# Attention's products by heads in column groups, an output stage with tokens on the rows, and other prices in the planner

## The chip, the cores and the metric

The kernel runs on one core of a Trainium2 chip. That core has TensorE (PE, matrix products into PSUM banks), VectorE (DVE), ScalarE (ACT), GpSimd (POOL) and the queue that issues DMA (SP). The metric is the device time of one execution in microseconds, the median of several runs; lower is better.

## The reference

Three stages follow each other: attention with 8 heads over 4 sequences of 512 local and 32 global tokens, a feed-forward layer, and a layer of 8 experts that all tokens pass through, weighted by a balanced gate.

```
s_g = scale * q_g @ k_all.T                    # global tokens see all
s_l = [scale * q_l @ k_g.T, where(|i-j| <= 32, scale * q_l @ k_l.T, -1e9)]
x = concat(softmax(s_g) @ v_all, softmax(s_l) @ v_all)      # 2176 tokens x 512
x = maximum(x @ w_in, 0) ** 2 @ w_out                       # 512 -> 2048 -> 512, float64 weights
P = exp(x @ w_gate - max); 8 times: rows / sum, columns / sum, * N / E
out = sum over e of P[:, e] * (maximum(x @ w1[e], 0) @ w2[e])   # 8 experts, 512 -> 1024 -> 512
```

## The kernel before

The 2176 tokens are 17 tiles of 128, in three blocks of 5, 6 and 6 tiles. Layer 0 is the feed-forward layer in 4 units of 512 hidden features, layer 1 the experts in 16 units (two an expert). A block passes through all units of a layer, then the next block does: 20 units for block 0, 40 for blocks 1 and 2.

Each product of float32 matrices is made of three products of float32r parts (a rounded part and the rest, `split_terms`). A unit has two halves. The hidden half makes hidden features from tokens by a scheme of seven products in place of eight on 2x2 blocks (Strassen-Winograd): `H(i, q)`, 14 groups of six products, 384 columns wide in blocks 1 and 2, 320 in block 0. The groups with bank a0 or a1 add up in one bank, and each is copied away (by ACT to `snaps`, or by DVE) before the next is added. `done` makes the hidden values. The output half differs:

- Block 0, `plain_unit`: it takes all eight blocks, works out the forms of the weights itself (`own_w1`, `own_w2`, on DVE, POOL and ACT) and stores them in HBM for the other blocks. In layer 1 the hidden values are the weights of the array, so a row of the result is a token, and DVE multiplies it by the token's probability while it adds it to `acc`.
- Blocks 1 and 2, `later_unit`: it loads the stored forms, makes forms of the hidden values (`form`, `combine`; s1 and s2 on DVE, s3 and s4 on POOL) and runs seven products by `O(name)`, each as two groups of six products of 384 columns, with tokens along the columns (turned). DVE adds each into `acc`. In layer 1 the hidden values are multiplied by the probabilities in `done`, since a column can't be scaled by a number per row; `turn_prob` turns the probabilities, writes them to HBM, and one DMA an expert spreads them over the rows (tile `tw1`). `send` turns each output tile back on PE at the end of a block.

Attention goes over 16 pairs of heads. `local` does two query tiles of a pair: scores with 64 rows a head, on the two halves of the array's rows, softmax on DVE, ACT and POOL, transposes, and the product with the values, in which one product of 256 columns makes both heads by each head's values and a half of the result is not used. `glob` does the global tokens of two pairs. `convert` turns the float64 words of `w_in` and `w_out` into float32 by integer operations on ACT, DVE and POOL and is run beside attention.

The order of all this is not written by hand. A `Recorder` takes every call with its operands, `cost` gives it a duration, and `plan` lists the operations by critical path on a model of the engines; what is emitted is each engine's list in that order. All instructions are therefore recorded with the recorder's line (L79, L84 in the changed kernel), and tiles name them: `a`, `b`, `d`, `y` are PSUM banks, `xf` and `c` the forms of tokens and of hidden weights, `xh` and `zs` hidden values (probabilities in attention), `wide` and `snaps` results on the way, `w`, `r`, `tw` output weights, `acc` the tokens.

## Time and profile before

| | |
|---|---|
| median of 3 runs (lowest, highest) | 2043.98 us (2042.07, 2045.91) |
| profiled execution, its span | 2047.04 us, 2045.3 us |
| PE busy | 1945.5 us, 95% of the span, 11008 products |
| weight loads (PEld) busy | 1828.0 us, 89% |
| DVE busy | 1722.7 us, 84%, 3171 instructions |
| ACT busy | 1003.2 us, 49% |
| POOL busy | 820.7 us, 40% |
| mean granted TensorE clock | 0.984 |

Busy PE time is modelled, and products overlap: the distance between starts, or a count in a stretch, says more than the duration of one. Durations of DVE and ACT instructions overlap by a little too. A product of float32 (in attention and the gate) leaves two records, one of float32r leaves one.

### The profile page before, as it was taken

How to read it: one execution, taken by the hardware profiler on the slowest of the kernel's cores; microseconds unless marked ns; L12 is line 12 of the kernel's file. 1: busy time of each engine (PE TensorE's matmuls, PEld its weight loads, DVE VectorE, ACT ScalarE, POOL GpSimd, SP SyncE). 2: the span in 40 equal slices, each digit the busy share in tenths (PEclk: the TensorE clock that was granted, in tenths of full speed). 3: DMA queues.
4: the chain of work that ended last, by engine and by line, in shares of the span. 5: the costliest groups of instructions: out<-in, count | busy, mean ns of one | idle time of the engine just before them, and what ended most of it. 6: DMA issues, size and time to landing. Idle time of an engine off the chain costs nothing.

```text
span 2045.3 us, 32874 instructions
## 1 busy us (share of the span) xinstructions
PE 1945.5 (95%) x11008; PEld 1828.0 (89%) x11008; DVE 1722.7 (84%) x3171; ACT 1003.2 (49%) x2319; POOL 820.7 (40%) x843
## 2 busy tenths in 40 slices
PE   7899999999988999999999999999999999999998
PEld 5677889999986888888889999999999999999998
DVE  4788998676798878888878899889899889989987
ACT  5788755676564444554445333333334433433432
POOL 4466653333352545455434233323323323333331
PEclk8999999999989999999999999999999999999999
DMA  8877789666635888788898777777676767677763
GB/s 194 225 200 202 237 272 326 223 219 227 226 127 192 275 296 281 266 275 273 299 308 273 238 233 235 245 228 234 232 234 222 250 233 253 217 244 234 234 225 103
DMA packets 335930, 486.21 MB, mean 238 GB/s; under 512 B 91400, under 2 KB 252168, under 8 KB 335760
## 3 DMA queue, kind: packets, MB, share of 16 engines
q1 hardware_dynamic: 335760, 484.10, 72.8%
q8 instruction: 87, 1.43, 0.3%
q14 instruction: 83, 0.68, 0.1%
HBM read 351.03 MB, written 128.24 MB: 234 GB/s over the span
## 4 chain that ended last, share of the span: by engine, by line
PE 55%; DVE 27%; DMA 5%; issue 4%; ACT 2%; POOL 1%; SPq 0%; DVEq 0%; ACTq 0%; POOLq 0%
PE y L79 26%; PE a L79 14%; PE d L79 10%; DVE wide L79 10%; DVE xh L79 8%; PE b L79 5%; DMA r<-in_moe_w_dram 2%; DVE xf L79 2%; DVE zs L79 2%; DVE r L79 2%; DVE acc L79 1%; DVE c L79 1%; ACT xh L79 1%; DMA w2forms<-xf 1%; DVE ss L79 1%
## 5 line engine op out<-in xcount | busy, mean ns | idle before, releaser
L79 PE MATMUL a<-xf,c 128*128 128x384 f32 (+1 forms) x2880 | 549.4, 333 | 35.9 <-DVE zs L79 20.6
L79 PEld LDWEIGHTS a<-xf,c 128*128 128x128 f32 x2880 | 486.5, 191 | 55.8 <-DVE zs L79 25.3
L79 ACT CAST xh<-wide 128x384 fp32r<-128x384 f32 x480 | 239.1, 514 | 348.2 <-DVE wide L79 278.0
L79 POOL TENSOR_TENSOR c<-r,c 128x256 fp32r<-128x256 f32 (+1 forms) x160 | 185.9, 1166 | 550.5 <-ACT c L79 512.4
L79 POOL TENSOR_TENSOR wide<-wide 128x384 f32<-128x384 f32 (+1 forms) x192 | 248.2, 1298 | 286.3 <-DVE xh L79 72.0
L79 DVE TENSOR_TENSOR xh<-wide,xh 128x384 fp32r<-128x384 f32 x480 | 325.8, 700 | 34.5 <-ACT xh L79 34.5
L79 PE MATMUL d<-xf,c 128*128 128x384 f32 (+1 forms) x1440 | 277.6, 329 | 0.3 <-DMA c<-w1forms 0.2
L79 DVE TENSOR_TENSOR acc<-y,acc 128x384 f32<-128x384 f32 (+2 forms) x401 | 214.4, 548 | 41.2 <-PE y L79 40.4
L79 PEld LDWEIGHTS d<-xf,c 128*128 128x128 f32 x1440 | 244.1, 189 | 1.1 <-DVE wide L79 0.5
L79 PE MATMUL y<-w,xh 128*128 128x512 f32 x960 | 222.7, 392 | 1.0 <-DVE acc L79 1.0
L79 PE MATMUL y<-xh,w 128*128 128x384 f32 (+1 forms) x1104 | 206.6, 331 | 13.1 <-DVE xh L79 10.1
L79 PEld LDWEIGHTS y<-w,xh 128*128 128x128 f32 x960 | 180.4, 189 | 38.4 <-DVE acc L79 1.4
L79 ACT CAST c<-r 128x512 fp32r<-128x512 f32 (+1 forms) x240 | 121.0, 512 | 175.7 <-PE b L79 151.0
L79 PEld LDWEIGHTS y<-xh,w 128*128 128x128 f32 x1104 | 182.3, 189 | 25.4 <-DVE xh L79 22.3
L79 DVE SCALAR_TENSOR_TENSOR wide<-wide,tw 128x384 f32<-128x384 f32 x192 | 182.2, 951 | 4.3
L79 PE MATMUL b<-xf,c 128*128 128x384 f32 (+1 forms) x720 | 139.2, 328 | 0.8 <-DVE wide L79 0.8
L79 PE MATMUL y<-xh,r 128*128 128x384 f32 x720 | 139.5, 335 | 0.0
L79 ACT COPY snaps<-a 128x384 f32<-128x384 f32 (+1 forms) x240 | 109.9, 458 | 49.5 <-PE a L79 42.8
L79 POOL TENSOR_TENSOR w<-r,w 128x512 fp32r<-128x512 f32 x40 | 54.5, 1364 | 197.5 <-ACT w L79 129.7
L79 PEld LDWEIGHTS y<-xh,r 128*128 128x128 f32 x720 | 126.1, 188 | 0.0
L79 PEld LDWEIGHTS b<-xf,c 128*128 128x128 f32 x720 | 121.5, 188 | 1.2 <-DVE wide L79 1.2
L79 ACT CAST w<-r 128x512 fp32r<-128x512 f32 x80 | 47.9, 621 | 146.0 <-PE y L79 123.2
(154 smaller groups left out, 3220.7 us busy)
## 6 DMA issues: line engine op xcount, KB each, us to landing
c<-w1forms SPq DMA_DIRECT2D x160, 512.0 KB, 4.4
w<-w2forms SPq DMA_DIRECT2D x160, 512.0 KB, 4.3
r<-in_moe_w_dram SPq DMA_DIRECT2D x128, 512.0 KB, 4.8
w1forms<-c SPq DMA_DIRECT2D x80, 512.0 KB, 5.3
w2forms<-xf SPq DMA_DIRECT2D x160, 256.0 KB, 4.2
r<-w2forms SPq DMA_DIRECT2D x80, 512.0 KB, 4.3
w2forms<-w SPq DMA_DIRECT2D x240, 128.0 KB, 4.1
tw<-w2forms SPq DMA_DIRECT2D x40, 512.0 KB, 4.4
```

The costliest lines, as they stand in the source:

```text
L79: getattr(getattr(self.nc, eng), name)(*args, **kwargs)
```

## The change

Five things change.

1. In attention the product with the values makes each head by itself: `local` runs pairs of products of 128 columns, one with its result on PSUM rows 0 to 63 and one on 64 to 127; `glob` does the same by pairs of heads in the scores and by four heads in the product with the values. The result is then one block, and one eviction on DVE moves it, where an eviction by ACT and one by DVE moved the halves.
2. The output half of `later_unit` in layer 1 has tokens on the rows, as block 0 has: `O_tokens` with products of 256 columns. DVE multiplies by the probability at the eviction. `turn_prob`, its DMAs and the transposes of `send` go, and ACT alone makes the hidden values.
3. s3 and s4 of `later_unit` are on DVE, in both layers.
4. One cast of `convert` goes from ACT to POOL (32 times).
5. The planner: `cost` says of each operation whether it uses the port that DVE and POOL share, and `listed` lengthens two that overlap; durations of DVE, ACT and POOL count 1.05 times, a DMA lands 4 us later, grouped products side by side count a half or a quarter, and there are four rounds for three.

```diff
+        for op in self.ops:
+            if op.eng == "sync":
+                op.lat += LATER
+            elif op.eng in ("vector", "scalar", "gpsimd"):
+                op.dur *= SLOWER
+        order, _, _ = plan(self.ops)
...
+        op.dur = dur * {"heads": 0.5, "scores": 0.5, "heads4": 0.25}.get(tag, 1.0) + (0.25 if tag else 0.0)
...
+        if not psum and name in ("tensor_scalar", "tensor_copy", "memset"):
+            return 0.15 + 0.00053 * n, 0.09, 0, True
+        d = 0.149 + 0.00105 * n
+        if name == "scalar_tensor_tensor" and psum and n == 512:
+            d += 0.06
+        return d, 0.09, 0, kinds.count("SB") > 1
     if name in ("tensor_scalar", "memset", "tensor_copy", "affine_select"):
-        return 0.33 + 0.00056 * n, 0.09, 0
-    return 0.25 + 0.0023 * n, 0.09, 0
+        return 0.33 + 0.00053 * n, 0.09, 0, True
+    return 0.19 + 0.00215 * n, 0.09, 0, True
...
+SLOWER, LATER = 1.05, 4.0
...
+def slowed(dur, beside, eng):
+    if beside <= 0:
+        return dur
+    rate = 0.64 if eng == "vector" else 0.78
+    return dur / rate if dur <= beside * rate else dur + beside * (1 - rate)
...
+        if nodes[i][3]:
+            d = slowed(d, held["gpsimd" if e == "vector" else "vector"] - t, e)
+            held[e] = t + d
...
-        act.activation(out=up, in_=lower, func=AF.Copy, scale=2.0**-29)
+        pool.tensor_scalar(out=up, in0=lower, scalar1=2.0**-29, scalar2=0.0, op0=mul, op1=add)
...
+            pv = pv_bank()[:, 0 : 2 * P].rearrange("p (t n) -> p t n", t=2)
+            with nc.group("heads"):
                 for t in range(2):
                     qt = 2 * qp + t
                     for y, (a, c) in enumerate(((va[:, qt], ta[:, t]), (vb[:, qt], tb[0:96, t]))):
...
-                        pe.matmul(pv[:, t].rearrange("p j q -> p (j q)"), lhsT=a, rhs=c, start=(y == 0), stop=(y == 1))
-            c0 = b * SL + qp * 2 * P
-            for j, r in enumerate(halves):
-                eng = (act, dve)[j]
-                if block_of(c0 // P) == block_of(c0 // P + 1):
-                    blk = block_of(c0 // P)
-                    o = c0 - TBS[blk][0] * P
-                    dst = turned_block(blk)[r, p, o : o + 2 * P].rearrange("p (t q) -> p t q", t=2)
-                    move(eng, dst, pv[r, :, j, :])
-                else:
-                    for t in range(2):
-                        token_out(p, r, c0 + t * P, P, pv[r, t, j, :], eng)
+                        for j, r in enumerate(halves):
+                            pe.matmul(pv[r, t], lhsT=a[:, r], rhs=c[:, j], start=(y == 0), stop=(y == 1))
...
+            token_out(p, b * SL + qp * 2 * P, 2 * P, pv.rearrange("p t n -> p (t n)"), dve)
...
+            with nc.group("heads"):
+                for i in range(2):
+                    kt, o = KT[(n - 1 + i) % 3], slice(i * 2 * SG, (i + 1) * 2 * SG)
+                    w = bd[:, i].rearrange("p j s -> p (j s)")
+                    pe.matmul(sa[o], lhsT=w, rhs=kt[:, 0, 0 : P + SG], start=True, stop=True)
...
+            with nc.group("heads4"):
                 for y, (a, m) in enumerate(terms):
-                    pe.matmul(pv.rearrange("p h d -> p (h d)"), lhsT=a, rhs=m, start=(y == 0), stop=(y == len(terms) - 1))
+                    for h in range(4):
+                        i, j = divmod(h, 2)
+                        o = slice(h * SG, (h + 1) * SG)
+                        pe.matmul(pv[o], lhsT=a[:, o], rhs=m[:, i, halves[j]], start=(y == 0), stop=(y == len(terms) - 1))
...
-        pbc = TW[1].get(F32)[:, 0 : 2 * n]
-        if layer and u % UE == 0:
-            k = (tb - 1) * 2 * n
-            sp.dma_start(out=pbc, in_=turned_prob[e : e + 1, k : k + 2 * n].partition_broadcast(P))
...
+            act.activation(out=dst, in_=src, func=AF.Relu)
             if layer == 0:
-                act.activation(out=dst, in_=src, func=AF.Relu)
                 act.activation(out=dst, in_=dst, func=AF.Square)
-            else:
-                dve.scalar_tensor_tensor(
-                    out=dst, in0=src, scalar=0.0, in1=pbc[:, half * n : (half + 1) * n], op0=ALU.max, op1=mul
-                )
...
+            if layer:
+                return O_tokens(name, fm, wf)
...
+        def O_tokens(name, fm, wf):
+            for t in range(nj // 2):
+                z, w = bank[f"y{t}"], bank[("b", "d0", "d1")[t]]
+                ps = {"T1": w[:, HALF:DM], "B22": w[:, HALF:DM], "B21": w[:, 0:HALF]}.get(fm, z[:, 0:HALF])
+                with nc.group():
+                    k = 0
+                    for q in range(2):
+                        for lhs, rhs in split_terms(
+                            *(hidden_form(name, x, q)[:, t * P : (t + 1) * P] for x in range(2)), *(wf[:, x, q] for x in range(2))
+                        ):
+                            pe.matmul(ps, lhsT=lhs, rhs=rhs, start=(fm in ("B11", "T1") and k == 0), stop=(k == 5), skip_group_check=True)
+                            k += 1
+                if fm == "B21":
+                    continue
+                i, c, src = {
+                    "B11": (0, 0, ps), "T1": (1, 1, ps), "T2": (0, 1, ps), "T3": (1, 1, ps), "B22": (0, None, w), "T4": (1, 0, ps),
+                }[fm]
+                j = j0 + i * (nj // 2) + t
+                dst, pr = acc_t[:, j] if c is None else acc_t[:, j, c * HALF : (c + 1) * HALF], prob[:, j, e : e + 1]
+                if u == 0 and fm in ("B11", "T1", "T2", "T4"):
+                    dve.tensor_scalar(out=dst, in0=src, scalar1=pr, scalar2=None, op0=mul)
+                else:
+                    dve.scalar_tensor_tensor(out=dst, in0=src, scalar=pr, in1=dst, op0=mul, op1=add)
+                if u == NU[1] - 1 and fm in ("B22", "T4"):
+                    send(j)
...
-        s3 = lambda: combine("A11", "A21", sub, pool)
-        s4 = lambda: combine("A12", "A22", sub, pool)
+        s3 = lambda: combine("A11", "A21", sub, dve)
+        s4 = lambda: combine("A12", "A22", sub, dve)
...
+    def send(j):
+        if j * P < GL:
+            b, r = divmod(j * P, SL)
+            sp.dma_start(out=out[b * S + SG + r : b * S + SG + r + P], in_=acc_t[:, j])
+        else:
+            for b in range(B):
+                sp.dma_start(out=out[b * S : b * S + SG], in_=acc_t[b * SG : (b + 1) * SG, j])
...
-    def turn_prob():
-        for k in range(0, rest, 4):
-            nt = min(4, rest - k)
-            ps = y_bank()[0:E, 0 : nt * P]
-            with nc.group():
-                for j in range(nt):
-                    pe.transpose(ps[:, j * P : (j + 1) * P], prob[:, TBS[0][1] + k + j, :], ident)
-            act.copy(wide[0:E, k * P : (k + nt) * P], ps)
-        sp.dma_start(out=turned_prob, in_=wide[0:E, 0 : rest * P])
...
-    def send(tb, t, name):
-        x = turned_block(tb)
-        ps = bank[name].rearrange("p (c n) -> p c n", c=NC)
-        with nc.group():
-            for c in range(NC):
-                pe.transpose(ps[:, c], x[:, c, t * P : (t + 1) * P], ident)
-        dst = x[:, :, t * P : (t + 1) * P]
```

How the instructions stand on the engines, at three places.

DVE in a plain unit of layer 1, before: the first evictions of the hidden half (`zs1<-b`, `zs2<-a0`) and the forms of output weights (`r11<-r11`, `xf1<-r10`).

```order
L79 SCALAR_TENSOR_TENSOR xh1_171<-zs0_193,xh0_170 128x320
L79 TENSOR_TENSOR r11_198<-r11_198 128x256 x3
L79 TENSOR_TENSOR zs1_194<-b_89,snaps_77 128x320
L79 TENSOR_TENSOR xf1_66<-r10_197,xf0_65 128x512 x2
L79 TENSOR_TENSOR zs2_195<-a0_85,snaps_77 128x320
```

The same work after, in a unit of the same stretch:

```order
L84 TENSOR_TENSOR xf1_66<-r10_196,xf0_65 128x512 x2
L84 TENSOR_TENSOR r11_197<-r11_197 128x256
L84 SCALAR_TENSOR_TENSOR acc_63<-y1_91,prob_79,acc_63 128x512
L84 TENSOR_TENSOR r11_197<-r11_197 128x256 x2
L84 SCALAR_TENSOR_TENSOR acc_63<-y2_92,prob_79,acc_63 128x512
L84 TENSOR_TENSOR r11_197<-r11_197 128x256
L84 TENSOR_TENSOR c01_68<-tw0_191,c01_68 128x512
L84 SCALAR_TENSOR_TENSOR acc_63<-y0_90,prob_79,acc_63 128x512
L84 TENSOR_TENSOR c10_71<-tw1_120,c10_71 128x512
L84 TENSOR_TENSOR zs0_192<-b_89,snaps_77 128x320
```

The subtractions of `r11` stood in one row of three ahead of the first evictions of the hidden half; they now stand between evictions of output products (`acc<-y`), and the hidden half's first eviction (`zs0<-b`) comes after them.

PE where one later unit of layer 1 ends and the hidden half of the next begins, before (`y1<-xh4,r11` is the last output product, `xf` by `c` the hidden ones):

```order
L79 MATMUL y1_91<-xh4_173,r11_205 128x384
L79 MATMUL b_89<-xf0_65,c02_69 128x384
L79 MATMUL b_89<-xf1_66,c02_69 128x384
L79 MATMUL b_89<-xf0_65,c02_69 128x384 x2
L79 MATMUL b_89<-xf1_66,c02_69 128x384
L79 MATMUL b_89<-xf0_65,c02_69 128x384
L79 MATMUL a1_86<-xf0_65,c12_73 128x384
L79 MATMUL a1_86<-xf1_66,c12_73 128x384
L79 MATMUL a1_86<-xf0_65,c12_73 128x384 x2
L79 MATMUL a1_86<-xf1_66,c12_73 128x384
L79 MATMUL a1_86<-xf0_65,c12_73 128x384
L79 MATMUL d1_88<-xf0_65,c10_71 128x384
```

After, from the end of the next unit's product into d0 on:

```order
L84 MATMUL d0_87<-xf0_65,c00_67 128x384
L84 MATMUL b_89<-xf0_65,c02_69 128x384
L84 MATMUL b_89<-xf1_66,c02_69 128x384
L84 MATMUL b_89<-xf0_65,c02_69 128x384 x2
L84 MATMUL b_89<-xf1_66,c02_69 128x384
L84 MATMUL b_89<-xf0_65,c02_69 128x384
L84 MATMUL d1_88<-xf0_65,c10_71 128x384
L84 MATMUL d1_88<-xf1_66,c10_71 128x384
L84 MATMUL d1_88<-xf0_65,c10_71 128x384 x2
L84 MATMUL d1_88<-xf1_66,c10_71 128x384
L84 MATMUL d1_88<-xf0_65,c10_71 128x384
L84 MATMUL b_89<-xf0_65,c12_73 128x384
```

Before, the next unit's hidden half began with b, and the groups into a1 and d1 stood between its two groups into b. Now it begins with d0, directly behind the last output products, and only the group into d1 stands between the two into b.

PE in attention, the first product with the values, before and after (`xh` probabilities, `r10` and `w2` values):

```order
L79 MATMUL d0_87<-xh3_114,r10_125 128x256
L79 MATMUL d0_87<-xh5_116,w2_123 128x256
L79 MATMUL d0_87<-xh3_114,r10_125 128x256
L79 MATMUL d0_87<-xh5_116,w2_123 128x256
L79 MATMUL y1_91<-ident_64,xh1_112 128x128 x4
```

```order
L84 MATMUL y1_91<-ident_64,xh1_112 128x128 x4
L84 MATMUL d0_87<-xh3_114,r10_125 64x128 x2
L84 MATMUL d0_87<-xh5_116,w2_123 64x128 x2
L84 MATMUL d0_87<-xh3_114,r10_125 64x128 x2
L84 MATMUL d0_87<-xh5_116,w2_123 64x128 x2
L84 MATMUL y2_92<-ident_64,xh1_112 96x128 x4
```

Four products of 128 rows by 256 columns have become eight of 64 rows by 128 columns, two of a kind behind each other.

## Rows read from the trace of the kernel before

**Rows 1.** The page's first line.
```profile
span 2045.3 us, 32874 instructions
```

**Rows 2.** Busy us: PE, PEld, DVE, ACT, POOL (instructions); clock; DMA share; GB/s.
```profile
0.00:215.00 215.00, 188.09 (x1095) 149.60 (x1095) 158.56 (x529) 161.05 (x514) 124.11 (x231) 0.94 0.79 201
215.00:350.00 135.00, 122.98 (x784) 119.08 (x783) 125.41 (x205) 75.03 (x164) 70.41 (x63) 0.97 0.86 290
350.00:580.00 230.00, 225.14 (x1299) 219.31 (x1298) 161.32 (x287) 156.92 (x337) 83.30 (x69) 1.00 0.61 212
660.00:1050.00 390.00, 366.88 (x1971) 327.39 (x1970) 318.73 (x509) 188.35 (x407) 188.70 (x189) 0.99 0.83 282
1103.30:1521.80 418.50, 415.69 (x2354) 407.40 (x2353) 380.55 (x645) 156.21 (x339) 136.14 (x112) 1.00 0.72 235
```

**Rows 3.** Weight loads, 660 to 1050 us: busy, mean ns | idle before.
```profile
L79 PEld LDWEIGHTS a<-xf,c 128*128 128x128 f32 x651 | 102.5, 194 | 31.0 <-ACT snaps L79 18.0 <-DVE zs L79 11.7
```

**Rows 4.** PE's timeline in one plain unit of layer 1 (start, length).
```profile
874.37 1.04 PE L79 MATMUL a<-xf,c 128*128 128x320 f32 x6
875.24 1.04 PE L79 MATMUL d<-xf,c 128*128 128x320 f32 x6
...
884.10 1.15 PE L79 MATMUL a<-xf,c 128*128 128x320 f32 x6 [0.77 <-ACT snaps L79]
...
887.66 1.14 PE L79 MATMUL a<-xf,c 128*128 128x320 f32 x6 [0.66 <-DVE zs L79]
```

**Rows 5.** Timelines of POOL, DVE and ACT in that unit.
```profile
877.78 3.00 POOL L79 TENSOR_TENSOR r<-r 128x256 f32<-128x256 f32 x3
...
880.11 2.72 DVE L79 TENSOR_TENSOR r<-r 128x256 f32<-128x256 f32 x3
...
883.26 0.47 ACT L79 ACTIVATE xh<-zs 128x320 fp32r<-128x320 f32 x1 [1.82 <-DVE zs L79]
```

**Rows 6.** Timeline of PE in the attention stage.
```profile
107.88 1.03 PE L79 MATMUL a<-tw,snaps 64*128 64x224 f32 x8
108.84 1.09 PE L79 MATMUL y<-ident,xh 128*128 128x128 f32 x8
109.77 1.90 PE L79 MATMUL d<-xh,w 128*128 128x256 f32 x8
111.50 0.76 PE L79 MATMUL a<-tw,zs 128*128 128x160 f32 x3
```

**Rows 7.** Chain of waits, 0 to 215 us: shares.
```profile
by line: PE d L79 10.0%; ACT xh L79 8.0%; PE a L79 7.1%; PE y L79 4.0%; issue 3.8%; DVE wide L79 2.6%; DMA wide<-in_moe_w_in_dram 2.4%; DVE xh L79 2.3%; DMA wide<-in_moe_w_out_dram 2.3%; ACT wide L79 2.2%; PE b L79 1.9%; POOL xh L79 1.7%; D
```

**Rows 8.** PE's timeline at the gate: column groups, then tiny products.
```profile
389.77 0.64 PE L79 MATMUL d<-acc,gt 128*32 128x256 f32 x8
...
373.38 0.73 PE L79 MATMUL d<-picks,lt 128*128 128x8 f32 x6
```

**Rows 9.** Groups of equal shape: count | busy us, mean ns.
```profile
L79 DVE SCALAR_TENSOR_TENSOR wide<-wide,tw 128x384 f32<-128x384 f32 x192 | 182.2, 951 | 4.3
...
L79 DVE TENSOR_TENSOR acc<-y,acc 128x384 f32<-128x384 f32 x372 | 199.6, 550 | 37.2 <-PE y L79 36.6
...
L79 DVE TENSOR_TENSOR wide<-wide 128x384 f32<-128x384 f32 x160 | 102.7, 660 | 3.1 <-POOL wide L79 2.7
...
L79 DVE SCALAR_TENSOR_TENSOR acc<-y,prob,acc 128x512 f32<-128x512 f32 x70 | 52.4, 750 | 44.4 <-PE y L79 43.5
...
L79 DVE SCALAR_TENSOR_TENSOR wide<-a,tw 128x384 f32<-128x384 f32 x64 | 35.1, 548 | 0.0
```

**Rows 10.** The chain's end; PE's timeline at the turned probabilities.
```profile
2033.07 1.04 PE d L79 x6
...
2037.73 0.56 PE a L79 x3
...
2038.32 1.07 ACT acc L79 x2
...
654.43 2.73 PE L79 MATMUL y<-ident,prob 128*8 128x128 f32 x12 [1.17 <-DVE prob L79]
```

More of the change, by code (lines that the diff above doesn't have):

```diff
@@ L74, in emit @@
     def emit(self):
-        order, starts, span = plan(self.ops)
-        self.planned = starts, span
+        for op in self.ops:
[4 more added lines that the diff above has]
+        order, _, _ = plan(self.ops)
         for i in order:
@@ L181, in _add @@
             wr += [self.region(a) for a in outs]
+        if op.eng == "tensor":
+            for (outs, _), (_, _, _, kwargs) in zip(acc, calls):
+                (key, _), quads, _ = self.region(outs[0])
+                (rd if kwargs.get("start") is False else wr).append((("start of", key), quads, 1))
         for a in [a for outs, ins in acc for a in outs + ins]:
@@ L321, in graph @@
     return nodes, first, last
-def in_order(ops):
-    T, end, start, stall = {}, [], [], {}
-    nodes, first, last = graph(ops)
-    for i, (e, dur, deps) in enumerate(nodes):
-        t = max([T.get(e, 0.0)] + [end[j] + l for j, l in deps])
-        start.append(t)
-        end.append(t + dur)
-        T[e] = t + dur
-    return [start[f] for f in first], [end[l] for l in last], max(end)
+def slowed(dur, beside, eng):
[3 more added lines that the diff above has]
+    return dur / rate if dur <= beside * rate else dur + beside * (1 - rate)
 def listed(nodes, prio, back=False):
@@ L338, in listed @@
     left = [0] * n
-    for i, (_, _, deps) in enumerate(nodes):
+    for i, (_, _, deps, _) in enumerate(nodes):
         for j, l in deps:
@@ L355, in listed @@
     start = [0.0] * n
+    held = {"vector": 0.0, "gpsimd": 0.0}
     done = 0
@@ L674, in attention @@
         pool.memset(gz, 0.0)
-        for t in OG:
-            pool.memset(t, 0.0)
+        pool.memset(bd, 0.0)
         def turn_global(name):
@@ L735, in pv_bank, with token_out @@
             return bank[f"d{ring('pv', 2)}"]
[L737 removed]
+        def token_out(c, tok, n, src, eng):
             while n:
@@ L742, in token_out @@
                 k = min(n, t0 + TBS[tb][1] * P - tok)
-                move(eng, turned_block(tb)[rows, c, tok - t0 : tok - t0 + k], src[:, 0:k])
+                move(eng, turned_block(tb)[:, c, tok - t0 : tok - t0 + k], src[:, 0:k])
                 src = src[:, k:]
@@ new lines, in glob @@
+            with nc.group("heads"):
+                for i in range(2):
+                    kt, o = KT[(n - 1 + i) % 3], slice(i * 2 * SG, (i + 1) * 2 * SG)
+                    w = bd[:, i].rearrange("p j s -> p (j s)")
+                    pe.matmul(sa[o], lhsT=w, rhs=kt[:, 0, 0 : P + SG], start=True, stop=True)
+                for i in range(2):
+                    kt, o = KT[(n - 1 + i) % 3], slice(i * 2 * SG, (i + 1) * 2 * SG)
+                    w = bd[:, i].rearrange("p j s -> p (j s)")
+                    pe.matmul(sbk[o].rearrange("p (t n) -> p t n", n=P), lhsT=w, rhs=kt[:, 1:NQ, 0:P], start=True, stop=True)
@@ L1170, in done @@
             dst = h[HOMES[name]][q]
-            half = QUARTER_TOKENS[name]
             if other is not None:
```

126 lines of the change are left out of this document (44 added, 82 removed).

## The prediction

> **What bounds the kernel now.** I read the busy time per stretch first, then what the weight loads waited for, then single timelines at the waits, and the groups of equal shape for prices. The span is 2045.3 us [rows 1], and the profiled execution took 2047.04 us, 3.06 us above the median of the three runs, 2043.98 us. I make the sum against the profiled one and carry the difference in us to the median.
>
> The program has three kinds of stretch [rows 2]. In 0 to 215 us attention runs with the conversion of the float64 weights beside it: PE 188 us busy, ACT 161, DVE 159, and DMA at 0.79 of its time. No engine is full, and the chain of waits goes from engine to engine: PE's products into the banks d0 and d1 (probabilities times values) are its largest share, 10.0% or 21.5 us, the products into a0 and a1 7.1%, ACT on the probabilities 8.0% [rows 7]. In the plain units, which token block 0 uses, DVE is the fullest after PE (319 of 390 us in layer 1, 125 of 135 in the stretch with layer 0's), and PE waits before products: 31.0 us of idle time ahead of the loads for the a banks alone, 18.0 of it for ACT's copies and 11.7 for DVE [rows 3]. In the later units, 1103.3 to 1521.8 us holds fourteen of them, 168 products each (2354 records for 2352), so 29.9 us a unit. Six products of 384 columns take 1.04 us [rows 10], 0.173 each, and 168 of those are 29.06 us. So a later unit loses only 0.83 us to waits, and DVE is busy 27.2 us of it (380.55/14). These units are bound by the number and width of their products, with DVE close behind.
>
> **The later units of layer 1 (32 of them).** The hidden half keeps its 84 products of 384 columns. The output half goes from 84 of 384 columns to 126 of 256: seven products, three token tiles, six terms. The columns are the same, 32,256, but each product carries a fixed part. At 2.4 GHz 384 columns are 160 ns and the row gives 173; 320 columns are 133 ns, and six of them take 0.87 us (874.37 to 875.24), 146 each [rows 4]. The fixed part is 13 ns at both widths, so I take 256 columns (107 ns) as 120 ns. Per unit 126 x 0.120 - 84 x 0.173 = +0.59 us, and over 32 units +19 us. The trace has no such product at 256 columns. Its bounds are 107 ns, the columns alone, and 146, the next wider product: -33 and +124 us.
>
> What hides under a product is the load of the next 128 columns of weights. Six products of 8 columns take 0.73 us from the first start to the last end [rows 8], at most 0.122 each with almost nothing to multiply: the load alone. Under 173 ns that is covered with room; under 120 it is about even.
>
> DVE in such a unit: eight operations that multiply the hidden values by the probability go (six at 951 ns, two at 548), and so do fourteen additions of 384 columns at 550: 14.5 us. Eighteen evictions come that multiply by the probability and add, fifteen of 256 columns and three of 512. The 512-wide one has a row, 750 ns; for 256 I take 0.45, between two thirds of the 548 row (0.37) and the whole of it. Four subtractions of 660 ns come over from POOL [rows 9]. Sum 0.45 x 15 + 0.75 x 3 + 0.66 x 4 = 11.6 us, 2.9 fewer (1.4 to 4.1). DVE falls to some 24 of 30 us a unit, and POOL, which shares the work on SBUF with it, is rid of four operations. ACT, 156 of 418 us, takes eight more activations and has the room.
>
> New waits: the second output product may not start before the first has opened its bank, and the banks b, d0, d1 stay taken from the second output product to the sixth, whose eviction is the 512-wide one. Behind it in PE's order stand eighteen products of 256 columns (2.2 us) and then the next unit's first product into d0; three evictions of 0.75 us are 2.25. The cover is about even. Also, the next unit's two products into b now have one group (1.04 us) between them where two stood. Against this stands the lighter DVE. I let the waits fall from 0.83 to 0.4 us a unit, -14 us (bounds: all 27 us go, or as much comes back as the two thin covers, 0.7 us a unit, +22). Together: +5 us.
>
> **The turned outputs that go.** Twelve transposes of the probabilities stand in PE's order from 654.43 to 656.8 us with 1.17 us of wait ahead [rows 10]: -3 us. Forty-eight transposes in the sending of twelve tiles go, at 0.93/8 = 0.116 us (108.84 to 109.77) [rows 6]: -5.5 us of PE, of which the last stand at the end; behind them 1.07 us of ACT's copies go [rows 10], less an eviction that stays. Together -9 us (bounds -11 and -5: with the cover of other waits, the mid-program part is not got back).
>
> **Plain units.** Their code is unchanged; the planner's prices change: operations with two SBUF operands on DVE and POOL now lengthen each other, all three engines count 5% longer, and DMA lands 4 us later. The profile shows that the old prices were wrong just where PE waits. In the unit at 874 us DVE runs three subtractions of 256 columns for 2.72 us beside POOL's own, 0.91 each [rows 5], where the row of 384 columns at 550 ns [rows 9] gives 0.37 by width. Behind them ACT waits 1.82 us for DVE and is late with a copy, and PE stands 0.77 us at 884.10 for ACT and 0.66 at 887.66 for DVE [rows 4, 5]. In the changed order those subtractions stand between two evictions of outputs, with no hidden value behind them (the rows of DVE in the section on the change). I take half of the 31.0 us, -15 (bounds 0 and -31), and for the four plain units of layer 0, where DVE is 125 of 135 us [rows 2] and can give little, -4 (0 and -8).
>
> **Attention.** Per step of two query tiles the product with the values goes from eight records of 256 columns, 1.73 us (109.77 to 111.50; 0.85 ns a column), to sixteen of 128 in pairs on the two halves of the columns. That column groups run together the gate shows: eight records of 256 columns in four groups within 0.64 us [rows 8], against 1.73 in one. So 0.87 us would be left, but the scores, which use row halves, take 0.96 (107.88 to 108.84) for eight records in pairs of 224 columns, 0.76 us [rows 6]: I add 0.2 for going in and out, and 0.66 us is saved, 32 times, 21 us. In the eight global steps the scores are 2 x 2 records of 544 columns, 1.85 us, and halve; the product with the values is ten records of 256, 2.2 us, and becomes quarters side by side, of which I take 1.0 with its going in and out. That is 0.7 + 1.2 us a step, 15 us. TensorEngine Tiling (Array Packing) in the Trainium skill, Key Properties, says that a change of tiling mode drains TensorE; the 0.2 us beside it agree, and without it attention's saving on PE would be 28 us for 21.
> Of these 36 us only what lies on the chain counts: its share on the d banks is 21.5 us, of which 0.66/1.73 is 8; of 15.3 us on the a banks some 4. ACT loses 32 casts and the evictions of one half, POOL takes the casts on and has 91 us free. DVE's 159 us stay, and DMA's 0.79. I take -12 (bounds 0, DVE and DMA decide; -25, DVE then 84% busy).
>
> **Layer 0's later units** get the four subtractions, 2.6 us of DVE a unit, beside 161 of 230 us busy [rows 2]: hidden in DVE's idle time, 0 (bound +21 without that cover).
>
> **Sum.** -12 - 15 - 4 + 5 - 9 + 0 = -35 us: 2012 profiled, 2009 in the median.
>
> **Rivals.** (1) Weight loads set the pace of the 256-column products. 32 x 126 = 4,032 products: each ns more is 4 us, so from 129 ns on the gain is gone; at 133 it is 2061 us. Against it: the fixed part of 13 ns at both widths. For it: a load of up to 122 ns. Chance 0.11.
> (2) Waits only move: attention is held by DVE and DMA, the plain units lose as much at other places, the d0 wait appears. What is left is the turning and part of the rest: 2025 to 2043. Chance 0.22.
> (3) The waits go nearly whole, -31 in the plain units, -27 in the later ones, -20 in attention: 1970 to 1990. Chance 0.14.
> (4) The fixed part shrinks with the width. With the columns alone, 107 ns, 4,032 products take 52 us less than at 120: 1957 us. Both widths in [rows 4, 10] speak against it. Chance 0.03. TensorE: Matmul & The Clock Gate in the Trainium skill, section Back-to-back issue gap, gives N/2.4 + 2.5 ns, which would be an estimate of 109 ns here and a sum of 1965 us; at 320 and 384 columns the trace has 10 ns more than that.
>
> **Numbers.** The forecast, 1990 to 2025, has 0.50. The range leaves out (4), most of (1) and the outer part of (3): 1972 to 2041. A measurement of this kernel can tell about 0.2%, 4 us, from no change. Faster: the forecast, (3), (4), most of (2) and the mild part of (1), 0.83. Same 0.06, slower 0.11.
>
> **What would show it.** Right: six products of 256 columns in 0.72 us; a later unit of layer 1 at 29.8 to 30.3 us; DVE there near 80%; idle time ahead of the a banks' loads in the plain units near 15 us, and a plain unit of layer 1 near 27 us for 28; two products with the values starting within some 70 ns of each other; the end of attention 10 to 15 us earlier. Wrong: a 256-column pace above 0.125, a wait of PE for DVE's eviction of d0 in each unit, or plain units still at 28 us.

## The result and the profile after

The changed kernel took 1991.64 us in the median of four runs (1988.83 to 1992.21), the kernel before 2044.7 beside it; the ratio is 0.9739, 95% interval 0.9723 to 0.9756. That is 2.6% faster, and it lies in the predicted range, 17 us under the predicted time. How the gain is spread over the program is not what was predicted.

The page after, span and busy shares, in answer to [rows 1]:

```profile
span 1989.2 us, 36193 instructions
PE 1906.4 (96%) x12788; PEld 1810.0 (91%) x12788; DVE 1636.1 (82%) x3210; ACT 1074.0 (54%) x2456; POOL 652.7 (33%) x714
PE 83%; DVE 8%; DMA 2%; POOL 2%; issue 2%; ACT 1%; SPq 1%; DVEq 0%; ACTq 0%; POOLq 0%
```

The last line is the chain that ended last, by engine: PE now makes up 83% of it (on the page of before 55%, and DVE 27%). The same stretches as in [rows 2] (plain units and later units of layer 1 cut to where they now lie; columns as there):

```profile
0.00:215.00 215.00, 174.02 (x1679) 132.74 (x1679) 165.76 (x532) 140.78 (x452) 145.56 (x258) 0.91 0.79 200
215.00:350.00 135.00, 113.33 (x690) 110.66 (x691) 127.52 (x193) 65.86 (x138) 75.20 (x67) 0.89 0.85 289
350.00:580.00 230.00, 226.27 (x1304) 221.50 (x1303) 173.96 (x320) 159.36 (x345) 44.29 (x40) 0.99 0.63 213
660.00:1000.00 340.00, 339.65 (x1875) 306.54 (x1874) 307.30 (x494) 182.09 (x392) 187.75 (x182) 1.00 0.91 309
1093.00:1449.40 356.40, 356.40 (x2522) 356.40 (x2521) 283.56 (x552) 176.95 (x384) 57.62 (x48) 1.00 0.71 231
```

In layer 1, plain units (fourth line) and later ones (fifth) no longer leave PE idle: 0.35 us of 340, and nothing of 356.4, where [rows 2] had 23 of 390 and 2.8 of 418.5. The first two stretches look different: PE has less to do, 174 us where it had 188, but in 215 to 350 us it stands for 22 us, at a granted clock of 0.89 (0.97 before), beside a DVE busy 127.5 of 135 us.

To compare runs I cut each span at three starts on PE: the first product into bank b of layer 1's first plain unit, of its first later unit, and of its last unit. The changed kernel moves 42 output products of plain units, 0.228 us each, behind the second cut; such products are counted here with the plain units, in every run that has them.

| us | to layer 1 | plain units | later units | tail | span |
|---|---|---|---|---|---|
| before | 590.8 | 481.7 | 935.7 | 37.0 | 2045.3 |
| after | 589.5 | 439.2 | 927.9 | 32.6 | 1989.2 |
| difference | -1.3 | -42.5 | -7.8 | -4.4 | -56.1 |

Three quarters of the gain lie in the plain units of layer 1, whose operations the change does not touch.

### The profile page after: what moved, and what is told of

It reads as the page before. It is cut to its first block, busy times and chain, and to the rows that moved or that the text cites. A ratio compares the mean times of both kernels' runs of the same rounds, so it can differ in the third digit from the quotient of the medians.

```text
span 1989.2 us, 36193 instructions
## 1 busy us (share of the span) xinstructions
PE 1906.4 (96%) x12788; PEld 1810.0 (91%) x12788; DVE 1636.1 (82%) x3210; ACT 1074.0 (54%) x2456; POOL 652.7 (33%) x714
## 4 chain that ended last, share of the span: by engine, by line
PE 83%; DVE 8%; DMA 2%; POOL 2%; issue 2%; ACT 1%; SPq 1%; DVEq 0%; ACTq 0%; POOLq 0%
PE y L84 31%; PE a L84 23%; PE d L84 19%; PE b L84 10%; DVE wide L84 2%; DVE xh L84 2%; DVE zs L84 1%; POOL xh L84 1%; SPq L84 1%; DMA wide<-in_moe_w_out_dram 1%; DMA wide<-in_moe_w_in_dram 1%; DVE c L84 1%; ACT xh L84 1%; DVE xf L84 1%; POOL wide L84 1%
## 5 line engine op out<-in xcount | busy, mean ns | idle before, releaser
L84 PEld LDWEIGHTS a<-xf,c 128*128 128x128 f32 x2880 | 484.3, 190 | 20.9 <-DVE zs L84 12.3
L84 POOL TENSOR_TENSOR c<-r,c 128x512 fp32r<-128x512 f32 (+1 forms) x160 | 189.3, 1186 | 902.3 <-ACT c L84 708.0
L84 PE MATMUL y<-w,xh 128*128 128x512 f32 (+1 forms) x1536 | 303.6, 352 | 0.0
L84 PEld LDWEIGHTS y<-w,xh 128*128 128x128 f32 x1536 | 250.4, 190 | 35.9
L84 DVE SCALAR_TENSOR_TENSOR acc<-y,prob,acc 128x256 f32<-128x256 f32 (+1 forms) x436 | 224.8, 522 | 54.2 <-PE y L84 52.2
L84 ACT ACTIVATE wide<-wide 128x384 f32<-128x384 f32 (+1 forms) x336 | 179.5, 539 | 54.5 <-DVE wide L84 31.6
L84 DVE TENSOR_TENSOR wide<-wide 128x384 f32<-128x384 f32 x320 | 190.0, 612 | 6.6 <-ACT wide L84 3.6
L84 ACT CAST c<-r 128x512 fp32r<-128x512 f32 x240 | 121.0, 513 | 37.7 <-PE b L84 28.6
L84 PE MATMUL y<-xh,w 128*128 128x320 f32 (+1 forms) x528 | 94.0, 335 | 18.7 <-DVE w L84 11.8
L84 PE MATMUL d<-w,xh 128*128 128x256 f32 (+1 forms) x960 | 107.3, 271 | 1.2 <-DVE xh L84 1.2
L84 PEld LDWEIGHTS y<-xh,w 128*128 128x128 f32 x528 | 88.3, 202 | 21.1 <-DVE w L84 12.5
```

The source lines that it names most:

```text
L84: getattr(getattr(self.nc, eng), name)(*args, **kwargs)
```

## The experiments

Each kernel was timed in three rounds beside the kernel before, whose medians there were 2042.43 to 2044.25 us. The stretches are cut in the same way. The expectations speak of the raw stretch of the plain units, from cut to cut; with the moved products (all but e2, e7, e8, e12 and e13 have them) it is 9.6 us shorter than the table's, in e1 13.7.

| us | median | ratio, interval | to layer 1 | plain | later | tail |
|---|---|---|---|---|---|---|
| e1 planner alone | 2030.05 | 0.994 (0.992, 0.997) | 603.2 | 440.9 | 943.3 | 40.8 |
| e2 old prices | 2029.98 | 0.994 (0.991, 0.996) | 600.9 | 470.9 | 922.8 | 32.1 |
| e3 turned outputs | 1999.88 | 0.979 (0.976, 0.982) | 588.7 | 442.0 | 927.7 | 41.5 |
| e4 old attention | 1996.54 | 0.977 (0.975, 0.980) | 591.8 | 440.2 | 927.3 | 32.6 |
| e6 s3, s4 on POOL | 1994.48 | 0.976 (0.974, 0.978) | 595.1 | 436.4 | 926.7 | 34.0 |
| e7 no port rule | 1984.78 | 0.971 (0.969, 0.973) | 582.9 | 443.8 | 924.7 | 32.6 |
| e8 no slack | 2048.84 | 1.003 (1.001, 1.004) | 619.5 | 471.2 | 924.7 | 31.4 |
| e9 square on ACT | 1979.33 | 0.968 (0.966, 0.970) | 577.5 | 439.6 | 927.3 | 32.6 |
| e10 transfers 4 us late only | 1987.82 | 0.972 (0.969, 0.974) | 593.2 | 437.9 | 924.3 | 32.8 |
| e11 before, with slack | 2026.78 | 0.991 (0.988, 0.993) | 601.7 | 444.3 | 941.0 | 40.1 |
| e12 square on ACT, no port rule | 1975.05 | 0.965 (0.962, 0.968) | 576.1 | 442.1 | 924.6 | 32.6 |
| e13 transfers 2 us late | 2004.67 | 0.982 (0.980, 0.983) | 595.2 | 452.4 | 923.2 | 31.4 |

Every edit makes the planner write another order, so a few us in one stretch may be luck; a stretch that agrees to 5 us over eleven orders (later units at 922.8 to 927.9) is less likely to be.

**First: planner, turning and attention apart.** e1 has the operations of before in an order by the whole new planner (item 5), so of the change it keeps these lines and their functions:

```diff
+SLOWER, LATER = 1.05, 4.0
...
+        if nodes[i][3]:
+            d = slowed(d, held["gpsimd" if e == "vector" else "vector"] - t, e)
...
+def plan(ops, rounds=4, log=None):
```

e2 is the reverse, the changed operations at the prices of before (`cost_old`):

```diff
+    return (*cost_old(eng, name, outs, ins, kwargs, rec), False)
-SLOWER, LATER = 1.05, 4.0
+SLOWER, LATER = 1.0, 0.0
-def plan(ops, rounds=4, log=None):
+def plan(ops, rounds=3, log=None):
-        op.dur = dur * {"heads": 0.5, "scores": 0.5, "heads4": 0.25}.get(tag, 1.0) + (0.25 if tag else 0.0)
+        op.dur = dur
```

> The kernel before with the new planner alone (prices, shared port, slack, four rounds, order of opening a bank); no operation changes. Theory P (the gain in layer 1's plain units, some 50 us, comes from the order that the new prices make): 1995 to 2005 us, plain units of layer 1 at about 27 us. Theory T (it comes from the work that went, the turning and DVE's multiplications): 2030 to 2045 us, plain units at 28 to 30.

> The changed kernel with the old prices in the planner: no shared port, no slack, three rounds, products side by side not discounted; the dependence on the product that opens a bank stays, since the new output stage needs it. Theory P: 2030 to 2045 us, waits of PE for DVE and ACT back in the plain units. Theory T: 1990 to 2000 us.

The plain units follow the prices: 440.9 with the new ones and old operations, 470.9 with the old prices and new operations. So there e1 and e2 fit theory P, but their totals say that neither half gives more than some 0.6% in all. In e1 24 of the plain units' 41 us are lost again elsewhere: 12 up to layer 1, 8 in the later units, 4 in the tail.

e3 takes back item 2 (the turned output half, `turn_prob` and the transposes of `send`), e4 items 1 and 4 (attention and the cast), with all else as changed. The core of e3, then of e4:

```diff
-            act.activation(out=dst, in_=src, func=AF.Relu)
+                dve.scalar_tensor_tensor(
+                    out=dst, in0=src, scalar=0.0, in1=pbc[:, half * n : (half + 1) * n], op0=ALU.max, op1=mul
+                )
...
-            if layer:
-                return O_tokens(name, fm, wf)
```

```diff
-                        for j, r in enumerate(halves):
-                            pe.matmul(pv[r, t], lhsT=a[:, r], rhs=c[:, j], start=(y == 0), stop=(y == 1))
+                        pe.matmul(pv[:, t].rearrange("p j q -> p (j q)"), lhsT=a, rhs=c, start=(y == 0), stop=(y == 1))
...
-        pool.tensor_scalar(out=up, in0=lower, scalar1=2.0**-29, scalar2=0.0, op0=mul, op1=add)
+        act.activation(out=up, in_=lower, func=AF.Copy, scale=2.0**-29)
```

> The changed kernel with the turned output half of before in layer 1's later units (products of 384 columns, probabilities in the hidden half, turned probabilities, transposes at the end); the rest stays changed. Theory P: the loss is small, 5 to 15 us (1997 to 2007): products 19 us shorter, but waits, transposes and tail back. Theory T: 30 us or more (2020 to 2040).

> The changed kernel with attention's products, evictions and the cast of before. Theory G (attention ends 20 us earlier, but layer 0's plain units, held by DVE, give it all back): within 5 us of the changed kernel, 1988 to 1997. Theory A (attention's gain reaches the end): 2004 to 2012.

Theory P holds in e3, theory G in e4. Turning costs 8 us, most of it in the tail: 41.5 for 32.6. Attention's new products are worth some 5 us (1996.54 and 1991.64, and the two intervals, 0.975 to 0.980 and 0.972 to 0.976, touch), although its last product of PE comes 10 us earlier (201.5 for 211.8).

**Which of the prices.** e7 plans without lengthening on the shared port:

```diff
-        if nodes[i][3]:
+        if False:
             d = slowed(d, held["gpsimd" if e == "vector" else "vector"] - t, e)
```

e8 plans without slack; e10 with `SLOWER, LATER = 1.0, 4.0`, the transfers' lateness alone, and e13 with `1.0, 2.0`:

```diff
-SLOWER, LATER = 1.05, 4.0
+SLOWER, LATER = 1.0, 0.0
```

> The changed kernel, planned without the rule that two operations with two SBUF operands on DVE and POOL lengthen each other; the price table, the 5% and the 4 us of slack stay. Theory M (this rule is what took the waits out of layer 1's plain units, as the prediction argued from the slow subtractions): the stretch of those units, 430 us in the changed kernel and 482 before, goes back to 465 or more, total 2020 to 2035. Rival S (the slack did it): the stretch stays near 430 and the total within 8 us of 1992. Rival T (neither alone, the rest of the table does): also near 1992, here and in the run without the slack.

> The changed kernel, planned with the shared-port rule but without slack: no 5% on the engines, no 4 us on the transfers. Theory M: the plain stretch of layer 1 stays near 430 us, total within 8 us of 1992. Rival S (slack did it): the stretch goes back to 465 or more, 2020 to 2035, with waits of PE for transfers or for engines a little late at many places. Rival T: near 1992 here and without the port rule.

Theory M, which is the reason that the prediction gave for the plain units, falls: without the port rule the plain units stay at 443.8 and the total is even 7 us lower. Without the slack the whole gain is gone, 2048.84 us: plain units at 471.2, and the time up to layer 1 is 619.5, 30 us more. Without the slack the other edits together gain nothing: from layer 1 on they win 27 us, and ahead of it they lose 29. Theory S, that the slack did it, had the stretch right; the total is above its 2020 to 2035.

> The changed kernel planned with transfers that land 4 us later, but without the 5% on the engines. Without both it took 2048.8 us, its plain units of layer 1 479 us (430 in the changed kernel). Theory L (the lateness of transfers is the part that counts: loads and stores are issued earlier): stretch 425 to 440, total 1985 to 2000. Rival F (the 5% counts, engines planned a little slow get their work earlier): stretch 465 or more, total 2030 or more.

> The changed kernel planned with transfers 2 us late, half of the 4, and no 5%. With 0 it took 2048.8 us (plain stretch 471), with 4 it took 1987.8 (428). The plan counts a weight block of 512 KB as landed 3.4 us after its issue (1.8 and 524,288 bytes at its 330 KB a us); in layer 1's plain units it took 5.5 to 6.2, so 2 to 3 us more. Theory L (the plan's error in these transfers is the cause, and a lateness of its size mends it): at least two thirds of the 61 us come, 2008 or less, stretch 443 or less. Rival (it isn't the error but a wide lead that counts): half or less, 2018 or more.

It is the lateness of transfers, and the 5% isn't needed (the 5% alone was not run): without the 5%, 0, 2 and 4 us of lateness give 2048.84, 2004.67 and 1987.82 us, and 471.2, 452.4 and 437.9 in the plain units. Layer 1 begins at 619.5, 595.2 and 593.2 us, so ahead of it the first 2 us do nearly all. In the total two us bring 72% of what four bring, as theory L expected; in the plain units 56%, a raw stretch of 452.4 where 443 or less was expected. That 2 us is the error and 4 a safety beyond it is therefore not shown; that the lateness carries the gain is. What it changes on the engines shows in the same stretch of e8, e13 and e10, 640 to 1000 us. First e8: ACT's casts of loaded weights with the idle time ahead of them, the issue of these loads with the us to their landing, and PE's weight loads for the a banks:

```profile
L84 ACT CAST w<-r 128x512 fp32r<-128x512 f32 x48 | 28.9, 621 | 77.5 <-PE y L84 54.9 <-DMA r<-in_moe_w_dram 20.5 <-DMA w2forms<-w 1.4
L84 ACT CAST c<-r 128x512 fp32r<-128x512 f32 x24 | 14.9, 622 | 9.8 <-DMA r<-in_moe_w_dram 9.8
r<-in_moe_w_dram SPq DMA_DIRECT2D x50, 512.0 KB, 5.9
L84 PEld LDWEIGHTS a<-xf,c 128*128 128x128 f32 x576 | 92.2, 197 | 24.2 <-ACT snaps L84 14.2 <-DVE zs L84 8.7
```

Then the casts and the weight loads in e13:

```profile
L84 ACT CAST w<-r 128x512 fp32r<-128x512 f32 x52 | 32.1, 623 | 66.7 <-PE y L84 53.4 <-DMA r<-in_moe_w_dram 12.6
L84 PEld LDWEIGHTS a<-xf,c 128*128 128x128 f32 x636 | 97.0, 188 | 12.9 <-ACT snaps L84 7.0 <-DVE zs L84 4.6
```

And in e10:

```profile
L84 ACT CAST w<-r 128x512 fp32r<-128x512 f32 x52 | 30.6, 618 | 39.0 <-PE y L84 37.4 <-DMA r<-in_moe_w_dram 1.0 <-DMA w1forms<-c 0.4
L84 PEld LDWEIGHTS a<-xf,c 128*128 128x128 f32 x642 | 99.3, 189 | 3.8 <-ACT snaps L84 0.7 <-DVE zs L84 0.7 <-DVE xh L84 0.5
```

ACT's wait for weight blocks ahead of its casts to `w` goes 20.5, 12.6, 1.0 us, and PE's wait ahead of the a banks goes along: 24.2, 12.9, 3.8. How one wait becomes the other stands in e8's timelines at 780 us, SP's issue, ACT, then PE:

```profile
776.05 1.08 SPq L84 DMA_DIRECT2D r<-in_moe_w_dram  x1
...
778.29 1.14 SPq L84 DMA_DIRECT2D r<-in_moe_w_dram  x2
```

```profile
776.70 0.43 ACT L84 COPY snaps<-d 128x320 f32<-128x320 f32 x1 [0.45 <-PE d L84]
782.19 1.14 ACT L84 CAST w<-r 128x512 fp32r<-128x512 f32 x2 [5.06 <-DMA r<-in_moe_w_dram]
783.24 0.47 ACT L84 ACTIVATE xh<-zs 128x320 fp32r<-128x320 f32 x1
783.61 0.41 ACT L84 COPY snaps<-a 128x320 f32<-128x320 f32 x1
```

```profile
777.38 1.04 PE L84 MATMUL a<-xf,c 128*128 128x320 f32 x6
...
780.02 1.04 PE L84 MATMUL b<-xf,c 128*128 128x320 f32 x6
784.07 1.15 PE L84 MATMUL a<-xf,c 128*128 128x320 f32 x6 [3.00 <-ACT snaps L84]
```

The load is issued at 776.05 and lands 6 us later. ACT's next instruction is the cast that needs it, and ACT stands 5.06 us. Behind the cast in ACT's order is the copy of an a bank that PE finished 5 us before (its products start at 777.38); it comes at 783.61, and PE, which needs the bank free, stands 3.00 us. The profile names ACT as the releaser, and ACT was not busy: it was queued behind a load that had not landed.

How far off was the plan? It has a block of 512 KB land 3.8 us after the start of its issue (0.4 for the issue, 524,288 bytes at 330 KB a us, and 1.8), and to that it adds the time for which transfers wait for each other. So the 3.4 us of e13's expectation, without issue and queue, can't be set against the page's 5.9. The plan that e8's kernel.py makes has its 50 loads land after 4.9 us in the median, and this one after 4.7, with the cast right behind it. It took 6.0, so the way from issue to landing gives 1.3 of ACT's 5.06 us. The larger part is an issue that came late: the plan has it 4.3 us ahead of ACT's copy of the d bank, the timelines 0.65 (776.05 and 776.70). With 4 us more in the plan the cast stands further back in ACT's order, behind such copies, or the load further forward.

In the kernel before, this path is a small part. The row of the same casts from 640 to 1000 us has 8.0 us of waits for loads, where PE waits 28.2 us ahead of the a banks:

```profile
L79 ACT CAST w<-r 128x512 fp32r<-128x512 f32 x48 | 28.8, 621 | 116.4 <-PE y L79 104.5 <-DMA r<-in_moe_w_dram 8.0 <-DMA w2forms<-xf 2.4
```

That the lateness takes PE's waits away is shown; that most of them came about in this way is shown for none but e8.

**Slack on the operations of before.** e11 is the kernel before with the slack and nothing else:

```diff
+        for op in self.ops:
+            if op.eng == "sync":
+                op.lat += 4.0
+            elif op.eng in ("vector", "scalar", "gpsimd"):
+                op.dur *= 1.05
         order, starts, span = plan(self.ops)
```

> The kernel before, with nothing changed but the slack: 5% on DVE, ACT and POOL and 4 us on every transfer in the plan, at the old prices. Theory S2 (slack alone takes the waits out of the plain units, whatever the operations and the rest of the prices): the plain stretch of layer 1 falls from 482 to 440 or less, total 2000 to 2025. Rival (the old price table spoils it): the stretch stays at 460 or more, total within 10 us of 2044.

The plain units fall to 444.3, 37 us less, with old prices and old operations: the slack alone does that. PE's waits ahead of the a banks, 28.2 us from 640 to 1000 us in the kernel before, are gone:

```profile
L84 PEld LDWEIGHTS a<-xf,c 128*128 128x128 f32 x642 | 98.1, 188 | 2.1 <-DVE xh L84 0.4
```

The total falls by 17 us only, to just above the expected 2000 to 2025. As in e1, the later units are the other side, 941.0. e6 helps to say why: the changed kernel with s3 and s4 given back to POOL.

```diff
-        s3 = lambda: combine("A11", "A21", sub, dve)
-        s4 = lambda: combine("A12", "A22", sub, dve)
+        s3 = lambda: combine("A11", "A21", sub, pool)
+        s4 = lambda: combine("A12", "A22", sub, pool)
```

> The changed kernel with the four subtractions that make S3 and S4 of a later unit given back to POOL. The prediction charged 2.6 us of DVE a unit for them and nothing in time. Theory N (nothing on either engine): 1988 to 1996, later units of layer 1 at 29.7 us as in the changed kernel. Rival Q (POOL takes them at over 1 us each and its two-operand work slows DVE's, which is what made the planner-alone run's later units 21 us longer than before's): later units at 30.2 or more, in layer 0 too, total 2003 to 2015.

Theory N holds, 926.7 in the later units. e3 has turned outputs and s3, s4 on DVE, 927.7; e1 and e11 have both old ways, 943.3 and 941.0. So either of the two edits is enough there, and the two together give no more. Where these 13 us lie, windows of 1100 to 1500 and 1500 to 1950 us show, of e11 first, then of e3 (columns as in [rows 2]):

```profile
1100.00:1500.00 400.00, 397.23 (x2250) 391.15 (x2248) 371.91 (x615) 148.36 (x314) 128.94 (x106) 1.00 0.72 237
1500.00:1950.00 450.00, 442.55 (x2491) 433.66 (x2491) 411.85 (x675) 180.31 (x380) 147.78 (x122) 0.99 0.70 232
```

```profile
1100.00:1500.00 400.00, 394.68 (x2252) 392.32 (x2251) 357.40 (x673) 160.75 (x331) 62.61 (x55) 1.00 0.73 237
1500.00:1950.00 450.00, 447.50 (x2555) 445.38 (x2554) 397.07 (x751) 182.33 (x378) 68.89 (x61) 1.00 0.72 236
```

In the first window PE has as many products in both; in the second it has 64 more in e3, 11 us at 0.173. DVE is nearly full in e11 (371.91 of 400 us) and, with s3 and s4 and 58 instructions more, 14.5 us less busy in e3. But these two kernels differ in prices and attention too. Only s3 and s4 differ between e6 and the changed kernel; the first window and DVE's split of the hidden forms there, of e6, then of the changed kernel:

```profile
1100.00:1500.00 400.00, 398.71 (x2816) 398.11 (x2816) 310.84 (x570) 199.35 (x440) 128.64 (x111) 1.00 0.68 231
...
L84 DVE TENSOR_TENSOR xh<-wide,xh 128x384 fp32r<-128x384 f32 x163 | 105.6, 675 | 31.4 <-ACT xh L84 30.1
```

```profile
1100.00:1500.00 400.00, 398.50 (x2814) 397.79 (x2813) 321.41 (x624) 201.64 (x438) 65.85 (x56) 1.00 0.71 232
...
L84 DVE TENSOR_TENSOR xh<-wide,xh 128x384 fp32r<-128x384 f32 x162 | 92.2, 587 | 2.9 <-ACT xh L84 1.7
```

The same subtraction takes 675 ns while POOL works on `wide` too, and 587 without. So 54 instructions more cost DVE 10.6 us, and PE has as many products either way. That DVE's load is what costs e1 and e11 their 13 us fits these rows, but no run shows it.

**Where attention's gain went.** DVE is nearly full between the end of attention and layer 0's later units. e9 takes one of its operations there away:

```diff
-                if other is None:
-                    act.activation(out=z, in_=ps, func=AF.Relu)
-                dve.scalar_tensor_tensor(out=z, in0=z, scalar=0.0, in1=z, op0=ALU.max, op1=mul)
+                act.activation(out=z, in_=src, func=AF.Relu)
+                act.activation(out=z, in_=z, func=AF.Square)
```

> The changed kernel, but the square of the hidden values in layer 0's four plain units is made by ACT (Relu, then Square) in place of one DVE operation of 674 ns, 32 times: 21 us less on DVE in the stretch of 200 to 345 us, where DVE is busy 138 of 145 us, and some 26 more on ACT, busy 71 of 145. Theory G (attention's 21 us earlier end is given back there because DVE is full): the first later unit of layer 0 starts 10 to 20 us earlier than at 344.9, total 1972 to 1983. Rival D (DMA at 0.87 of its time there, or the conversion's chain, sets the end): it starts within 4 us of 344.9, total 1988 to 1995.

Theory G holds: the first later unit of layer 0 starts at 331.7, 13 us earlier, and the total is 1979.33, 12 us lower. In the changed kernel DVE's tiles in the row of shares below have 47% of the chain that ended last from 200 to 345 us, PE's 34%, and from 235 to 263 us PE has no long piece of it (start, length, engine and tile):

```profile
by line: PE y L84 26.2%; DVE xh L84 11.8%; DVE zs L84 11.5%; issue 10.3%; DVE wide L84 7.1%; DVE c L84 6.2%; DVE xf L84 5.5%; PE a L84 5.0%; DMA w2forms<-xf 4.6%; DVE w L84 3.7%; PE d L84 2.6%; ACT w L84 1.2%; SPq L84 1.2%; DVE r L84 1.1%; 
...
235.12 2.08 DVE c L84 x3
237.80 1.48 DVE c L84 x2
242.92 1.06 issue
244.16 1.12 DVE w L84
245.28 1.45 DVE wide L84
...
250.55 0.94 DVE xh L84
252.37 1.57 DVE xh L84
258.46 1.25 DVE xh L84 x2
```

The stretch of 200 to 345 us in e9, where the changed kernel had PE busy 117.99, DVE 137.99 and ACT 70.92 us, at 0.88 of the clock:

```profile
200.00:345.00 145.00, 127.90 (x775) 122.70 (x774) 129.45 (x186) 100.53 (x219) 87.95 (x77) 0.94 0.90 307
```

PE is busy 10 us more, at a higher granted clock, with DMA at 0.90 of its time for 0.87: rival D falls. A part of the 12 us may still be the new order, since e7, which moves no work, comes to layer 1 6.6 us earlier.

**Both that were faster.** e12 joins the edits of e7 and e9:

```diff
-        if nodes[i][3]:
+        if False:
...
+                act.activation(out=z, in_=src, func=AF.Relu)
+                act.activation(out=z, in_=z, func=AF.Square)
```

> Both edits that were faster than the changed kernel, together: the square of layer 0's plain units on ACT (1979.3 alone) and the plan without the port rule (1984.8 alone). If they add: 1971 to 1976, the first later unit of layer 0 starting 14 to 18 us earlier than at 344.9. If both only give back the same wait in the stretch of 200 to 345 us, or if the plan without the port rule is luck that another order doesn't repeat: 1977 to 1988.

1975.05 us, ratio 0.9652 (0.9622 to 0.9681): the two nearly add (12.3 and 6.9 alone), and this version beats the changed kernel by 16.6 us. Its first later unit of layer 0 starts at 310.9, but before the plain units' last products, so that start tells nothing here; layer 1 starts 13 us earlier.

## Why the prediction came out as it did

The total was inside the range and the forecast's own band, 1990 to 2025. It came 17 us under the predicted time, but three of its terms are off by 13 to 25 us, and not in one direction: that the total came so near is in part luck.

- **Plain units of layer 1 (-15, and -3 for turning the probabilities; measured -42.5).** The step "I take half of the 31.0 us" failed, and so did its reason, that the old prices were wrong about the shared port. Rival (3) had the waits go nearly whole, and here they did, though it names no reason. The row that answers to [rows 3], 660 to 1000 us after:

```profile
L84 PEld LDWEIGHTS a<-xf,c 128*128 128x128 f32 x624 | 95.8, 188 | 3.3 <-ACT snaps L84 0.9 <-DVE zs L84 0.2
```

  The 31.0 us were also not all: PE's idle time between the two cuts fell from 38.7 us (481.7 less 443.0 busy) to 8.0, its busy time from 443.0 us to 431.2 with the moved products, and a group of six products right behind a wait took 1.15 for 1.04 us [rows 4]. Of the three parts of the prices I costed the one for which I had rows, DVE's 0.91 us beside POOL [rows 5], and gave the 4 us of the transfers, named in the same sentence, no price. The runs showed that this part carries the gain: the plain units keep it without the port rule (e7, 443.8), without the 5% (e10, 437.9) and at the old prices with the slack (e11, 444.3), and lose it without the slack (e8, 471.2).

- **Attention (-12) and layer 0's plain units (-4): measured -1.3 up to layer 1.** Up to the first later unit of layer 0 it is even 2.9 us more (344.9 for 342.0). On PE the sizes were about right. The timeline after, in answer to [rows 6], the scores, the products with the values of a step, then of a global step in quarters:

```profile
94.75 1.03 PE L84 MATMUL a<-tw,snaps 64*128 64x224 f32 x8
95.71 1.10 PE L84 MATMUL d<-xh,w 128*64 128x128 f32 x16
96.74 1.42 PE L84 MATMUL y<-ident,xh 128*128 128x128 f32 x4
...
109.71 0.77 PE L84 MATMUL d<-w,xh 128*32 128x64 f32 x40
110.41 0.66 PE L84 MATMUL b<-ident,r 128*128 128x128 f32 x4
```

  A step's values take 1.03 us (95.71 to 96.74; 1.07 taken), a global step's 0.70 (1.0 taken). Attention ends 23 us earlier than before, 201.5 for 224.2. The gain is then lost: the bound that I named for it, "DVE and DMA decide", is what happened, and I gave it only a rival's weight. Rival (2) had the number of this stretch right. What I missed is the place: attention itself was not held. Behind it stand layer 0's plain units and the rest of the conversion, whose last operation on POOL ends at 303.4 us for 265.9, before a DVE that has 138 of 145 us to do.

- **Later units of layer 1 (+5; measured -7.8).** The pace was right: six products of 256 columns from 1980.99 to 1981.71, 0.120 us each, so rivals (1) and (4) fall together. TensorE: Matmul & The Clock Gate in the Trainium skill, section Back-to-back issue gap, would give an estimate of 109 ns by its formula for a single product by itself; the trace has 120, so the measurement decides.

```profile
1980.99 0.88 PE L84 MATMUL b<-r,xh 128*128 128x256 f32 x6
1981.71 0.88 PE L84 MATMUL d<-r,xh 128*128 128x256 f32 x6
```

  The products thus cost the 19 us (an estimate: 32 units of 126 at 0.120 for 84 at 0.173). What was mis-sized is the waits: I let them fall to 0.4 us a unit, and the twelve units of 1093 to 1449.4 us have none (29.70 us each, 2,520 products, the sums of their paces 29.65). The thin covers, d0 above all, held. DVE came out as costed, 80% (283.56 of 356.4); the 256-wide multiply-and-add took 0.48 us for the 0.45 taken:

```profile
L84 DVE SCALAR_TENSOR_TENSOR acc<-y,prob,acc 128x256 f32<-128x256 f32 x366 | 172.8, 480 | 40.4 <-PE y L84 38.6
L84 DVE TENSOR_TENSOR wide<-wide 128x384 f32<-128x384 f32 x320 | 190.0, 612 | 6.6 <-ACT wide L84 3.6
```

  By e3 the 19 us were not needed: turned outputs with s3 and s4 on DVE take 927.7 in the same units, their 29.06 us of products and some waits. In the later units the change to untransposed outputs gives nothing that moving s3 and s4 doesn't give.

- **Turning gone (-9; 8 by e3's total).** Right in size, not in place. Between e3 and the changed kernel 8.9 us lie in the tail, where the terms put some 4 (24 of the 48 transposes, and ACT's copies), and 2.8 in the plain units, where the probabilities were turned. But e3's tail, 41.5 us, is also longer than that of the kernel before, 37.0, so a part of the 8.9 is e3's order.

- **Layer 0's later units (0).** Their four subtractions hide as said: from the first later unit to layer 1 it is 244.6 us for 248.8 before.

What stays open: why e1 and e11 come to layer 1 12 to 14 us after the changed kernel, of which e4 (2.3) and e6 (5.6) account for 8 if they add; why the new prices without slack do worse than the old ones there (619.5 in e8, 600.9 in e2); by which path most of PE's waits in the plain units of before came about; and whether leaving out the port rule is a gain or one lucky order, since its 6.9 us in e7 lie up to layer 1, and of the 4.3 that it adds in e12 only 1.4 do.

## What to carry to other kernels

When a wait is put down to an engine that has time to spare, look at what that engine's queue stood behind: in e8's plain units ACT, busy 170 of 360 us, held PE up because the next cast in its order waited for a load that had not landed. Before pricing a planner's finer rules, give its transfers a margin: 4 us on each took 61 us off (e8 and e10), more than any rule about engines, and a load can be late at its issue as well as on its way. And a saving on the engine that the stage waits for is only worth what the next full engine leaves of it: attention's gain was lost in the stretch behind it, until DVE was relieved there.

## What was not expected of the hardware

Work that goes from POOL to DVE costs DVE much less than its own time: in the later units of the changed kernel four subtractions more a unit, at the 612 ns of its row above some 33 us of 400, add 10.6 us to DVE's busy time (321.41 for e6's 310.84), because its own subtractions get shorter, the split of the hidden forms 587 ns for 675. And a transfer's size says little of when it lands here: in e8's plain units stores of 128 KB and of 256 KB both landed 4.1 us after their issue, loads of 512 KB after 5.9.

```profile
w2forms<-xf SPq DMA_DIRECT2D x100, 256.0 KB, 4.1
...
w2forms<-w SPq DMA_DIRECT2D x145, 128.0 KB, 4.1
```
